# Projecting the late pairs' keys and queries in float32 from each head's own 64 rows

## The chip, the cores and the metric

The kernel runs on one core of a Trainium2 chip. The metric is the time of one execution on the device, in microseconds (us); a smaller one is better. The engines are PE (matrix multiplications, with PEld for its weight loads), DVE, ACT and POOL (arithmetic on vectors) and SP (which issues most of the transfers).

## The reference

Linear attention with a feature map, followed by a gated feed-forward network (FFN) over the heads put side by side. There are 8 batches, 8 heads, 576 tokens, 64 numbers a head; 128 features before the map's two signs; 4608 tokens of 512 go through an FFN of 1536.

```python
def phi(x):
    proj = np.einsum('bhsd,df->bhsf', x, w_phi)
    proj = proj - np.max(np.abs(proj), axis=-1, keepdims=True)
    return np.concatenate([np.exp(proj), np.exp(-proj)], axis=-1)
q_p, k_p = (phi(q), phi(k))
kv = np.einsum('bhsf,bhsd->bhfd', k_p, v)
z = np.sum(k_p, axis=2)
num = np.einsum('bhsf,bhfd->bhsd', q_p, kv)
den = np.einsum('bhsf,bhf->bhs', q_p, z)[..., None] + 1e-06
...
g = x @ w_gate
silu = g * (1.0 / (1.0 + np.exp(-g)))
val = x @ w_val
return (silu * val @ w_out).astype(np.float32)
```

The change concerns `proj`, the product of q and of k with `w_phi`, whose contraction is 64 long.

## The kernel before, in words

**Pairs.** Attention works on pairs of heads, 32 of them, numbered batch by batch. A pair's two heads lie one above the other: head 0 in rows (partitions) 0 to 63, head 1 in rows 64 to 127 of `kin` (keys) and `qin` (queries), tokens along the columns. The first 8 pairs are early, the other 24 late.

**Keys.** Tokens are cut into five blocks; four have 128 tokens of each head, and the fifth holds the last 64 tokens of both heads, each in its own rows with zeros beside them. Blocks 0 and 1, blocks 2 and 3, and block 4 are the three entries of `GROUPS`. An early pair multiplies a block of `kin` (the stationary operand) with `wbd`, 256 columns wide: `w_phi` twice on the diagonal, zeros elsewhere, so that one matmul over all 128 rows gives both heads' features. Block 4 goes with `wst`, `w_phi` twice one above the other. These operands are float32. Late pairs from pair 9 on split the keys: ACT copies them to a narrower format, float32r (`k_hi`, line 417), DVE takes the rest (`k_lo`, line 419), and three matmuls (high by high, high by low, low by high; lines 434 to 444) replace the float32 one. After the projection DVE takes the largest magnitude (`kmax`) and subtracts it (`ksub`), ACT takes two exponentials, and PE adds the values up in the bank `kv` (`values`, lines 463 to 474).

**Queries.** For late pairs the features lie in the rows and tokens in the columns. Each head's 64 rows are split into a high part (ACT, line 553) in its own rows and a low part (DVE, line 555) in the other head's rows, so that one matmul over 128 rows takes both parts; a second one has the weights' low part. Tokens come in two halves of 288 (`SH`), so a head has two steps of two matmuls, and each step's result is copied out by ACT (line 568). DVE then finds the largest magnitude over the features, ACT takes the exponentials, and PE multiplies them with the summed values (`numerators`, lines 612 to 620).

**FFN.** Tokens go in 12 chunks of 384. Chunks 0 to 5 use products of split float32r operands in three terms each (`first` into the banks `gv`, `second` into the banks `o`), chunks 6 to 11 go two at a time by a Strassen scheme (from line 976). In the late pairs' part of the program chunks 1 to 5 stand beside attention.

**Order.** The order is not that of the code. `Plan` (lines 65 to 165) holds steps, each with an engine, a cost in ns, the steps it waits for and a rank, and plays them through: an engine that is free takes the ready step of the lowest rank, and the instructions are written in that order. On PE attention ranks ahead of the FFN, whose steps fill what is left; if nothing is ready, a matmul of zeros (`nil`) is written. A step with `take` needs a bank of PSUM, a step with `give` returns it. There are two work banks, and for early pairs the three `o` banks besides.

Of the kernel before, what the change touches and what calls it, by code (L numbers as in the profile page):

```python
# [10 lines left out]
F32R = mybir.dt.float32r  # L11
# [6 lines left out]
P = 128  # L18
S = 576
# [45 lines left out]
class Plan:  # L65
# [28 lines left out]
    def run(self):  # L94
# [11 lines left out]
        def start(e):  # L106
            nonlocal n, wire
            held = []
            got = None
            while ready[e]:  # L110
                key, s = heapq.heappop(ready[e])
                if s.take is not None and not self.free and not (s.early and self.extra):
                    held.append((key, s))
                    continue
                got = s
                break
# [10 lines left out]
            s = got  # L127
            if s.take is not None:
                self.bank[s.take] = (self.extra if s.early and self.extra else self.free).pop(0)
            s.fn()  # L130
# [41 lines left out]
def dve(n):  # L172
    return 150 + 1.04 * n
# [10 lines left out]
def act(n):  # L184
    return 190 + 0.86 * n
# [11 lines left out]
def favor_attention_moe(ctx: ExitStack, tc: tile.TileContext, qT, kT, v, w_phi, wg, wv, wo, out):  # L197
# [10 lines left out]
    def sb(name, shape, dtype=F32, n=None):  # L208
        if n is None:
            return pool.tile(shape, dtype, name=name, tag=name)  # L210
        return [pool.tile(shape, dtype, name=f"{name}{i}", tag=f"{name}{i}") for i in range(n)]


    wbd_hi, wbd_lo = sb("wbd_hi", [P, 2 * NF], F32R), sb("wbd_lo", [P, 2 * NF], F32R)
    wst_hi, wst_lo = sb("wst_hi", [P, NF], F32R), sb("wst_lo", [P, NF], F32R)
    w1_hi = sb("w1_hi", [P, 2, NK, P], F32R, NFT)
# [26 lines left out]
    def view(tag, shape, dtype=F32, when=0, o=None):  # L243
        n = size(shape)
        if o is None:
            o = filled.get((tag, when), 0)
            filled[tag, when] = o + n
        assert o + n <= ROOM[tag], (tag, when, o + n)
        made = lambda: shaped(space(tag, when, F32 if dtype is U32 else dtype)[:, o:o + n], shape, dtype)
        return made if when else made()  # L250
# [3 lines left out]
    qx, qe = ([view("m1", [2, S]) for _ in range(2)] for _ in range(2))  # L254
    kp = [view("m1", [2, 2, 2, NF]) for _ in range(2)]
    kvs = [view("m2", [4 * P]) for _ in range(2)]
# [14 lines left out]
    we, wa = ([t[:, i * DM:(i + 1) * DM] for i in range(2)] for t in shared[2:])  # L271
    ks, qs = view("a1", [2, SK], F32R, 1), view("a1", [2, S], F32R, 1)
    for t, shape in ((kin, [SK]), (qin, [SK]), (vf, [5, 2, D2])):
# [20 lines left out]
    make_identity(nc, ident)  # L294
    for hi, lo, w in ((wbd_hi, wbd_lo, wbd), (wst_hi, wst_lo, wst)):
        nc.scalar.copy(hi, w)
        nc.vector.tensor_tensor(out=lo, in0=w, in1=hi, op=ALU.subtract)
    nc.gpsimd.memset(vf[0][:, :, :, D:], 1.0)
# [73 lines left out]
    def attention(i, rank):  # L372
        b, pr = divmod(i, NPAIR)
        plan.early = early = i < EARLY_PAIRS
        plain = i <= EARLY_PAIRS
        j = i % 2
# [36 lines left out]

        if plain:
            k_ready = k_in
        else:
            k_hi = add("ACT", act(SK), lambda: nc.scalar.copy(ks()[:, 0], get(kin[one])),
                       [*k_in, last.get(("khi", i - 1)), *weights_done], rk)
            k_lo = add("DVE", dve(SK), lambda: vec.tensor_tensor(
                out=ks()[:, 1], in0=get(kin[one]), in1=ks()[:, 0], op=ALU.subtract), [k_hi], rk)  # L420
            k_ready = [k_hi, k_lo]
            last["kin", i] = k_lo
        kv_steps = []
        for g, (t0, t1) in enumerate(GROUPS):

            tail = t1 == 5
            w = t1 - t0
            n = 1 if tail else 2 * w
            key = ("k", i, g)
            buf = (3 * i + g) % 2  # L430
            view = lambda key=key, n=n: work[plan.bank[key]][:, :n * NF].rearrange("p (n f) -> p n f", f=NF)
            room = kp[buf].rearrange("p t h s f -> p (t h) s f")[:, :n]

            def project(t0=t0, t1=t1, key=key, tail=tail):
                o = work[plan.bank[key]]
                for t in range(t0, t1):
                    c = slice(t * P, (t + 1) * P)
                    acc = o[:, :NF] if tail else o[:, (t - t0) * 256:(t - t0 + 1) * 256]
                    if plain:
                        matmuls([(acc, get(kin[one])[:, c], wst if tail else wbd, True, True)])  # L440
                    else:
                        khi, klo = (ks()[:, n, c] for n in range(2))
                        w_hi, w_lo = (wst_hi, wst_lo) if tail else (wbd_hi, wbd_lo)
                        matmuls([(acc, khi, w_hi, True, False), (acc, khi, w_lo, False, False), (acc, klo, w_hi, False, True)])

            width = NF if tail else 256
            kproj = add("PE", w * (pe32(width) if plain else 3 * pe(width)), project, k_ready, rk, take=key)
            m = km[(3 * i + g) % len(km)][:, :n]
# [13 lines left out]

            def values(t0=t0, t1=t1, room=room, tail=tail):
                kv_open[0] = not tail
                if tail:
                    for k in range(2):
                        nc.tensor.matmul(ps_kv[:, 2 * k * D2:2 * (k + 1) * D2], room[:, 0, k],  # L467
                                         get(vf[one])[:, 4].rearrange("p h d -> p (h d)"), start=False, stop=k == 1)
                    return
                for t in range(t0, t1):  # L470
                    for h in range(2):
                        for k in range(2):
                            o = ps_kv[:, (2 * k + h) * D2:(2 * k + h + 1) * D2]
                            nc.tensor.matmul(o, room[:, 2 * (t - t0) + h, k], get(vf[one])[:, t, h], start=t + h + k == 0, stop=False)  # L474

            kv = add("PE", 2 * n * pe32(D2), values, [e1, *v_in, last.get(("kv", i - 1)), *kv_steps[-1:]], rk)
            last["kp", 3 * i + g] = kv
            kv_steps.append(kv)
        last["khi", i] = kproj
        if plain:  # L480
            last["kin", i] = kproj
        last["vf", i] = kv_steps[-1]
# [18 lines left out]
        if early:  # L501
            for g, (t0, t1) in enumerate(GROUPS):
# [15 lines left out]

                pj = add("PE", pe32(NF) if tail else w * pe32(256), project, q_in, rank, take=key)
                mx = add("DVE", dve(u * NF), lambda u=u, m=m, view=view: vec.tensor_reduce(  # L520
# [16 lines left out]

                tn = add("PE", u * 108, turn, [qc], rank, take=key2)
                last["qy", n] = tn
# [9 lines left out]
        else:  # L549
            copies, q_lo = [], []  # L550
            for h in range(2):
                ra, rb = rows(h)
                hi = add("ACT", act(S), lambda h=h, ra=ra: nc.scalar.copy(qs()[ra, h], get(qin[one])[ra, :S]),
                         [*q_in, last.get(("qs", h, i - 1)), *weights_done], rq)
                lo = add("DVE", dve(S), lambda h=h, ra=ra, rb=rb: vec.tensor_tensor(
                    out=qs()[rb, h], in0=get(qin[one])[ra, :S], in1=qs()[ra, h], op=ALU.subtract), [hi], rq)
                q_lo.append(lo)
                for part in range(2):
                    key = ("q", i, h, part)
                    c = slice(part * SH, (part + 1) * SH)  # L560

                    def project(h=h, c=c, key=key):
                        acc = work[plan.bank[key]][:, :SH]
                        x = qs()[:, h, c]
                        matmuls([(acc, wst_hi, x, True, False), (acc, wst_lo, x, False, True)])

                    pj = add("PE", 2 * pe(SH), project, [lo], rq, take=key)
                    copies.append(add("ACT", act(SH), lambda h=h, c=c, key=key: nc.scalar.copy(
                        qx[j][:, h, c], work[plan.bank[key]][:, :SH]), [pj, *use("qx")], freeing, give=key))
                last["qs", h, i] = pj  # L570
            last["qin", i] = q_lo[-1]
            blocks = lambda t: flat(t).rearrange("p (a j) -> p a j", j=32)
# [10 lines left out]
            def over_groups():  # L583
# [6 lines left out]

            mx = [add("DVE", dve(S), f, [turns[h]], rm) for h, f in enumerate(per_head(largest))]
            mg = add("DVE", 6 * 170, over_groups, [*mx, last.get(("back", i - 1))], rm)
            back = [add("DVE", dve(S), f, [mg], rm) for f in per_head(lambda h: vec.transpose(
                blocks(qe[j], h), qu[:, cols(h)].rearrange("p (a o) -> p a o", o=1).broadcast_to([P, NBL, 32])))]
# [11 lines left out]
        for h in range(2):  # L606
            for part in range(2):
# [11 lines left out]

                nu = add("PE", 2 * pe32(SH), numerators, [*done[h], *kvc, nu], rn, take=key)  # L620
                free = last.get(("num", i - 1), ())
# [526 lines left out]
```

## Time and profile before

| what | value |
|---|---|
| median of 3 runs | 1263.96 us (1260.27 to 1263.97) |
| the profiled execution | 1263.36 us, span 1261.6 us, granted clock 0.997 |
| PE busy | 1240.2 us (98%), 7008 matmul passes |
| DVE busy | 942.8 us (75%) |
| ACT busy | 687.5 us (54%) |
| POOL busy | 241.5 us (19%) |
| the longest sum of PE waits on one line | 4.9 us in 3 waits (line 1008, for the DVE sums of line 1019) |

A row of the trace names the line, the engine, the operation, the tile written and the tiles read, and the shape. Several tiles share a space, so `m` stands for most tiles of attention and `a` for the split operands and the weights on their way. PE's matmuls overlap at their ends: an instruction's own length is longer than the distance to the next one's start, and that distance is what it costs while PE is busy. The page counts a float32 matmul as two passes and one of float32r as one.

### The profile page before, as it was taken

Reading aid. Unit: us, or ns where it says so; the run is one execution under the profiler, and the core shown is the slowest. Engines: PE = TensorE matmul, PEld = TensorE weight load, DVE = VectorE, ACT = ScalarE, POOL = GpSimd, SP = SyncE. Lnnn points to the kernel's source line nnn. Section 1 sums busy time; section 2 is a strip of 40 time slices with the busy share of each in tenths; the row PEclk is TensorE's granted clock in tenths of the full one; section 3 lists DMA queues with packets and bytes.
Section 4 is the critical chain, followed back from the end, with each engine's and each line's share of the span. In section 5 each row is a group of like instructions: output and inputs, shape, how many; then the busy total and the mean of one; then the engine's idle time right before and its main releaser. Section 6 shows DMA issues by size and latency. Waiting matters only on the chain.

```text
span 1261.6 us, 19300 instructions
## 1 busy us (share of the span) xinstructions
PE 1240.2 (98%) x7008; PEld 1145.5 (91%) x7008; DVE 942.8 (75%) x1674; ACT 687.5 (54%) x1419; POOL 241.5 (19%) x306
## 2 busy tenths in 40 slices
PE   9999999999999999999999999989999999999998
PEld 8887999999888998999999999979998999989997
DVE  7997799998899898999989632476557656575553
ACT  5887333336788787777778522233334433353333
POOL 0000000000000000000000010065565655565550
PEclk9999999999999999999999999999999999999999
DMA  4443355557554433343443244542213322222211
GB/s 137 135 116 99 132 176 173 178 167 211 164 153 123 130 92 114 117 121 114 141 118 97 86 152 151 175 150 76 71 55 111 117 73 76 75 101 75 76 51 51
DMA packets 107312, 149.26 MB, mean 118 GB/s; under 512 B 52048, under 2 KB 61776, under 8 KB 107216
## 3 DMA queue, kind: packets, MB, share of 16 engines
q1 hardware_dynamic: 106752, 147.76, 37.7%
q8 instruction: 55, 0.90, 0.3%
q14 instruction: 41, 0.34, 0.1%
q10 hardware_dynamic: 464, 0.26, 0.1%
HBM read 119.67 MB, written 28.31 MB: 117 GB/s over the span
## 4 chain that ended last, share of the span: by engine, by line
PE 89%; DVE 5%; DMA 2%; ACT 1%; POOL 1%; issue 1%; SPq 0%; DVEq 0%; ACTq 0%; POOLq 0%
PE gv L313 23%; PE gv L1008 19%; PE o L313 19%; PE work L313 17%; PE kv L474 8%; PE kv L313 2%; PE kv L467 1%; POOL a L915 1%; POOL a L920 1%; DVE m L953 0%; DVE xl L957 0%; PE o L536 0%; DMA x_dram<-m 0%; DVE m L525 0%; DMA out_dram<-osb 0%
## 5 line engine op out<-in xcount | busy, mean ns | idle before, releaser
L313 PE MATMUL gv<-xh,w_hi 128*128 128x384 f32 x576 | 200.6, 348 | 1.4 <-DVE th L744 1.4
L313 PE MATMUL gv<-xh,w_lo 128*128 128x384 f32 x576 | 193.3, 336 | 0.0
L313 PE MATMUL gv<-xl,w_hi 128*128 128x384 f32 x576 | 193.3, 336 | 0.0
L1008 PE MATMUL gv<-xh,m 128*128 128x384 f32 x504 | 150.6, 337 | 3.1 <-ACT m L1016 2.5
L915 POOL TENSOR_TENSOR a<-w_hi,m 128x256 f32<-128x256 f32 x48 | 40.3, 869 | 500.5 <-DMA m<-wlo_dram 492.7
L915 POOL TENSOR_TENSOR a<-w_hi,w_lo 128x256 f32<-128x256 f32 x96 | 85.7, 922 | 193.6 <-DMA w_lo<-wlo_dram 169.9
L920 POOL TENSOR_TENSOR a<-a 128x256 f32<-128x256 f32 x144 | 114.9, 798 | 8.5
L313 PEld LDWEIGHTS gv<-xh,w_hi 128*128 128x128 f32 x576 | 108.3, 188 | 5.1 <-DVE th L744 2.0
L313 PE MATMUL work<-m,m 128*128 128x288 f32 x408 | 110.2, 408 | 1.7 <-ACT m L624 1.7
L313 PE MATMUL o<-w_hi,hh 128*128 128x512 f32 x270 | 111.3, 412 | 0.0
L313 PEld LDWEIGHTS gv<-xl,w_hi 128*128 128x128 f32 x576 | 108.3, 188 | 3.1 <-DVE xl L659 0.2
L1019 DVE TENSOR_TENSOR a<-gv,a 128x384 f32<-128x384 f32 x72 | 39.9, 554 | 93.9 <-PE gv L1008 93.6
L313 PEld LDWEIGHTS gv<-xh,w_lo 128*128 128x128 f32 x576 | 108.1, 188 | 0.0
L313 PE MATMUL o<-w_hi,hl 128*128 128x512 f32 x270 | 107.2, 397 | 0.0
L1008 PEld LDWEIGHTS gv<-xh,m 128*128 128x128 f32 x504 | 93.2, 188 | 6.0 <-ACT m L1016 3.1
L313 PE MATMUL o<-w_lo,hh 128*128 128x512 f32 x243 | 95.7, 394 | 0.0
L313 PEld LDWEIGHTS work<-m,m 128*128 128x128 f32 x408 | 75.6, 190 | 19.2 <-ACT m L624 2.0
L742 ACT ACTIVATE th<-gv 128x384 f32<-128x384 f32 x72 | 35.3, 490 | 96.5 <-PE gv L313 93.4
L767 ACT CAST hh<-th 128x384 fp32r<-128x384 f32 x108 | 55.2, 511 | 52.5 <-DVE th L747 39.1
L474 PEld LDWEIGHTS kv<-m,m 128*128 128x128 f32 x640 | 75.9, 192 | 3.6 <-ACT m L458 1.2
L1008 PE MATMUL gv<-xh,w_hi 128*128 128x384 f32 x216 | 73.0, 338 | 4.9 <-DVE a L1019 4.9
L474 PE MATMUL kv<-m,m 128*128 128x66 f32 x640 | 75.5, 273 | 1.3 <-ACT m L458 1.0
(183 smaller groups left out, 2993.9 us busy)
## 6 DMA issues: line engine op xcount, KB each, us to landing
w_lo<-wlo_dram SPq DMA_DIRECT2D x60, 512.0 KB, 3.6
w_lo<-wlo_dram SPq DMA_DIRECT2D x78, 256.0 KB, 3.1
wlo_dram<-w_lo SPq DMA_DIRECT2D x36, 256.0 KB, 2.1
out_dram<-osb SPq DMA_DIRECT2D x30, 256.0 KB, 2.9
a<-in_wg_dram SPq DMA_DIRECT2D x12, 512.0 KB, 3.6
a<-in_wv_dram SPq DMA_DIRECT2D x12, 512.0 KB, 3.6
a<-in_wo_dram SPq DMA_DIRECT2D x12, 512.0 KB, 3.7
m<-wlo_dram SPq DMA_DIRECT2D x12, 512.0 KB, 3.5
```

Source lines behind the costliest of these rows:

```text
L313: nc.tensor.matmul(o, l, r, start=a, stop=z)
L467: nc.tensor.matmul(ps_kv[:, 2 * k * D2:2 * (k + 1) * D2], room[:, 0, k], get(vf[one])[:, 4].rearrange("p h d -> p (h d)"), start=False, st ...
L474: nc.tensor.matmul(o, room[:, 2 * (t - t0) + h, k], get(vf[one])[:, t, h], start=t + h + k == 0, stop=False)
L742: s1 = add("ACT", act(CH), lambda: nc.scalar.activation(t_, ps_gv[0][:, :CH], AF.Tanh, scale=0.5), [ends[0], th_free[j]], FIRST)
L767: s4 = add("ACT", act(CH), lambda: nc.scalar.copy(get(hh[b]), th[j]), [made, hid_free[b]], FIRST)
L915: gp.tensor_tensor(out=full()[:, block(n)], in0=hi[:, block(n)], in1=get(low)[:, block(n)], op=ALU.add)
L920: gp.tensor_tensor(out=x[:, block(o)], in0=x[:, block(l)], in1=x[:, block(r)], op=ALU.subtract)
L1008: nc.tensor.matmul(o[:, :CH], l, r, start=begin and i == 0, stop=i == len(terms) - 1, skip_group_check=True)
L1019: return add("DVE", dve(CH), lambda: vec.tensor_tensor(out=snap[n](), in0=bank_c[:, :CH], in1=snap[n](), op=ALU.add), after, FIRST)
```

## The change

Late pairs are no longer split. Keys of the four full blocks are projected by eight float32 matmuls, each over one head's 64 rows, against the 64 rows of `wst` that hold `w_phi` for that head; head 0's results go to one work bank, head 1's to the other, and heads alternate. Block 4 stays a matmul over 128 rows, now in float32. Queries are projected by float32 matmuls of 288 columns over one head's 64 rows, the two heads of a half in one step, again into two banks. The steps' list of banks (`take`) can now hold two, and a step whose banks are not free holds back all later ones that need banks. The four split copies of `w_phi`, the splits of keys and queries and their space go away. Pair 8 takes part too. The build gives a matmul over 64 rows its own strip of PE's array: size 64 by 128, at row 0 or row 64.

```diff
-                if s.take is not None and not self.free and not (s.early and self.extra):
+                if s.take is not None and (saved or len(s.take) > len(self.free) + (len(self.extra) if s.early else 0)):
                     held.append((key, s))
+                    saved = True
                     continue
...
-        if plain:
-            k_ready = k_in
-        else:
-            k_hi = add("ACT", act(SK), lambda: nc.scalar.copy(ks()[:, 0], get(kin[one])),
-                       [*k_in, last.get(("khi", i - 1)), *weights_done], rk)
-            k_lo = add("DVE", dve(SK), lambda: vec.tensor_tensor(
-                out=ks()[:, 1], in0=get(kin[one]), in1=ks()[:, 0], op=ALU.subtract), [k_hi], rk)
...
+                for t in range(4):
+                    for h in range(2):
+                        r = rows(h)[0]
+                        matmuls([(work[plan.bank["k", i, h]][:, t * NF:(t + 1) * NF], x[r, t * P:(t + 1) * P],
+                                  wst[r], True, True)])
+
+            if early:
+                kproj = add("PE", pe32(NF) if tail else 2 * pe32(256), project, k_in, rk, take=[key])
+            elif g != 1:
+                kproj = add("PE", n * pe32(NF), project,
+                            [*k_in, *(last.get(("kp", 3 * i + u - 2)) for u in ((2,) if tail else (0, 1)))], rk,
+                            take=[key] if tail else [key, ("k", i, 1)])
...
-            copies, q_lo = [], []
-            for h in range(2):
-                ra, rb = rows(h)
-                hi = add("ACT", act(S), lambda h=h, ra=ra: nc.scalar.copy(qs()[ra, h], get(qin[one])[ra, :S]),
-                         [*q_in, last.get(("qs", h, i - 1)), *weights_done], rq)
-                lo = add("DVE", dve(S), lambda h=h, ra=ra, rb=rb: vec.tensor_tensor(
-                    out=qs()[rb, h], in0=get(qin[one])[ra, :S], in1=qs()[ra, h], op=ALU.subtract), [hi], rq)
...
-                        matmuls([(acc, wst_hi, x, True, False), (acc, wst_lo, x, False, True)])
...
+            copies = [None] * 4
+            for part in range(2):
+                c = slice(part * SH, (part + 1) * SH)
+                keys = [("q", i, h, part) for h in range(2)]
+
+                def project(c=c, keys=keys):
+                    for h in range(2):
+                        r = rows(h)[0]
+                        matmuls([(work[plan.bank[keys[h]]][:, :SH], wst[r], get(qin[one])[r, c], True, True)])
+
+                pj = add("PE", pe32(SH), project, [*q_in, *use("qx")], rq, take=keys)
```

On PE, a query step of a late pair between the values' last matmuls and the FFN (`gv`) reads so before; `work` with a number is a work bank, `a` the split queries:

```order
L467 MATMUL kv<-m_0_105,m_0_104 128x132 x2
L313 MATMUL work_132<-a_1_2452,wst_hi 128x288
L313 MATMUL work_132<-a_1_2452,wst_lo 128x288
L313 MATMUL work_133<-a_1_2452,wst_hi 128x288
L313 MATMUL work_133<-a_1_2452,wst_lo 128x288
L313 MATMUL gv_129<-xh_98,w_hi_75 128x384
```

After the change the same place on PE has one matmul a head, and the values' matmuls between the two query steps; `m` is now `qin` itself:

```order
L308 MATMUL work_129<-m_0_101,wst 128x288
L308 MATMUL work_128<-m_0_101,wst 128x288
L460 MATMUL kv<-a_1_2516,m_0_100 128x132 x2
L308 MATMUL gv_125<-xh_94,w_hi_69 128x384
L308 MATMUL gv_125<-xl_97,w_hi_69 128x384
L308 MATMUL gv_125<-xh_94,w_lo_91 128x384
```

Four matmuls of two steps have become two of one step, and in a strip of 64 rows each.

On PE, the keys of a late pair before: the first of two such groups, six matmuls into one bank, and the start of the second:

```order
L313 MATMUL work_132<-wbd_hi,a_1_2452 128x256
L313 MATMUL work_132<-wbd_lo,a_1_2452 128x256
L313 MATMUL work_132<-wbd_hi,a_1_2452 128x256 x2
L313 MATMUL work_132<-wbd_lo,a_1_2452 128x256
L313 MATMUL work_132<-wbd_hi,a_1_2452 128x256
L313 MATMUL work_133<-wbd_hi,a_1_2452 128x256
```

And the keys of a late pair on PE after, from the FFN step ahead of them:

```order
L308 MATMUL gv_126<-xh_94,w_hi_69 128x384
L308 MATMUL gv_126<-xl_97,w_hi_69 128x384
L308 MATMUL gv_126<-xh_94,w_lo_91 128x384
L308 MATMUL work_129<-wst,m_0_101 128x128
L308 MATMUL work_128<-wst,m_0_101 128x128
```

The last two rows stand there four times in turn, once a block; all eight matmuls are one step that holds both banks, and FFN matmuls over all rows stand on both sides of it.

More of the change, by code (lines that the diff above doesn't have):

```diff
@@ L108, in start @@
             held = []
-            got = None
+            got, saved = None, False
             while ready[e]:
                 key, s = heapq.heappop(ready[e])
-                if s.take is not None and not self.free and not (s.early and self.extra):
+                if s.take is not None and (saved or len(s.take) > len(self.free) + (len(self.extra) if s.early else 0)):
                     held.append((key, s))
+                    saved = True
                     continue
@@ L127, in start @@
             s = got
-            if s.take is not None:
-                self.bank[s.take] = (self.extra if s.early and self.extra else self.free).pop(0)
+            for t in s.take or ():
+                self.bank[t] = (self.extra if s.early and self.extra else self.free).pop(0)
             s.fn()
@@ L211, in sb @@
         return [pool.tile(shape, dtype, name=f"{name}{i}", tag=f"{name}{i}") for i in range(n)]
-    wbd_hi, wbd_lo = sb("wbd_hi", [P, 2 * NF], F32R), sb("wbd_lo", [P, 2 * NF], F32R)
-    wst_hi, wst_lo = sb("wst_hi", [P, NF], F32R), sb("wst_lo", [P, NF], F32R)
     w1_hi = sb("w1_hi", [P, 2, NK, P], F32R, NFT)
@@ L254, in favor_attention_moe @@
     qx, qe = ([view("m1", [2, S]) for _ in range(2)] for _ in range(2))
-    kp = [view("m1", [2, 2, 2, NF]) for _ in range(2)]
+    kp = [view("m1", [4, 2, NF]) for _ in range(2)]
     kvs = [view("m2", [4 * P]) for _ in range(2)]
@@ L271, in favor_attention_moe @@
     we, wa = ([t[:, i * DM:(i + 1) * DM] for i in range(2)] for t in shared[2:])
-    ks, qs = view("a1", [2, SK], F32R, 1), view("a1", [2, S], F32R, 1)
     for t, shape in ((kin, [SK]), (qin, [SK]), (vf, [5, 2, D2])):
@@ L294, in favor_attention_moe @@
     make_identity(nc, ident)
-    for hi, lo, w in ((wbd_hi, wbd_lo, wbd), (wst_hi, wst_lo, wst)):
-        nc.scalar.copy(hi, w)
-        nc.vector.tensor_tensor(out=lo, in0=w, in1=hi, op=ALU.subtract)
     nc.gpsimd.memset(vf[0][:, :, :, D:], 1.0)
@@ L374, in attention @@
         plan.early = early = i < EARLY_PAIRS
-        plain = i <= EARLY_PAIRS
         j = i % 2
@@ L411, in attention @@
                      before("vf"), rank) for h in range(2)]
-        if plain:
-            k_ready = k_in
-        else:
-            k_hi = add("ACT", act(SK), lambda: nc.scalar.copy(ks()[:, 0], get(kin[one])),
-                       [*k_in, last.get(("khi", i - 1)), *weights_done], rk)
-            k_lo = add("DVE", dve(SK), lambda: vec.tensor_tensor(
-                out=ks()[:, 1], in0=get(kin[one]), in1=ks()[:, 0], op=ALU.subtract), [k_hi], rk)
-            k_ready = [k_hi, k_lo]
-            last["kin", i] = k_lo
-        kv_steps = []
+        kv_steps, kproj = [], None
         for g, (t0, t1) in enumerate(GROUPS):
             tail = t1 == 5
-            w = t1 - t0
-            n = 1 if tail else 2 * w
+            slots = [(4, 0)] if tail else [(t, h) for t in range(t0, t1) for h in range(2)] if early else \
+                [(t, g) for t in range(4)]
+            n = len(slots)
             key = ("k", i, g)
@@ L431, in attention @@
             view = lambda key=key, n=n: work[plan.bank[key]][:, :n * NF].rearrange("p (n f) -> p n f", f=NF)
-            room = kp[buf].rearrange("p t h s f -> p (t h) s f")[:, :n]
+            room = kp[buf][:, :n]
             def project(t0=t0, t1=t1, key=key, tail=tail):
[L435 to L447, printed above, removed]
+                x = get(kin[one])
+                if early or tail:
+                    o = work[plan.bank[key]]
+                    for t in range(t0, t1):
+                        c = slice(t * P, (t + 1) * P)
+                        matmuls([(o[:, :NF] if tail else o[:, (t - t0) * 256:(t - t0 + 1) * 256], x[:, c],
+                                  wst if tail else wbd, True, True)])
+                    return
+                for t in range(4):
[9 more added lines that the diff above has]
+                            take=[key] if tail else [key, ("k", i, 1)])
             m = km[(3 * i + g) % len(km)][:, :n]
@@ L461, in attention, with values @@
             last["km", 3 * i + g] = ksub
-            def values(t0=t0, t1=t1, room=room, tail=tail):
+            def values(g=g, slots=slots, room=room, tail=tail):
                 kv_open[0] = not tail
@@ L469, in values @@
                     return
-                for t in range(t0, t1):
-                    for h in range(2):
-                        for k in range(2):
-                            o = ps_kv[:, (2 * k + h) * D2:(2 * k + h + 1) * D2]
-                            nc.tensor.matmul(o, room[:, 2 * (t - t0) + h, k], get(vf[one])[:, t, h], start=t + h + k == 0, stop=False)
+                for m, (t, h) in enumerate(slots):
+                    for k in range(2):
+                        o = ps_kv[:, (2 * k + h) * D2:(2 * k + h + 1) * D2]
+                        nc.tensor.matmul(o, room[:, m, k], get(vf[one])[:, t, h], start=g + m + k == 0, stop=False)
             kv = add("PE", 2 * n * pe32(D2), values, [e1, *v_in, last.get(("kv", i - 1)), *kv_steps[-1:]], rk)
@@ L478, in attention @@
             kv_steps.append(kv)
-        last["khi", i] = kproj
-        if plain:
-            last["kin", i] = kproj
+        last["kin", i] = kproj
         last["vf", i] = kv_steps[-1]
@@ L517, in project @@
                                  (o[:, (t - t0) * 256:(t - t0 + 1) * 256], x, wbd, True, True)])
-                pj = add("PE", pe32(NF) if tail else w * pe32(256), project, q_in, rank, take=key)
+                pj = add("PE", pe32(NF) if tail else w * pe32(256), project, q_in, rank, take=[key])
                 mx = add("DVE", dve(u * NF), lambda u=u, m=m, view=view: vec.tensor_reduce(
@@ L536, in turn @@
                             nc.tensor.transpose(o[:, (h * w + t) * P:(h * w + t + 1) * P], y[:, 2 * t + h], ident)
-                tn = add("PE", u * 108, turn, [qc], rank, take=key2)
+                tn = add("PE", u * 108, turn, [qc], rank, take=[key2])
                 last["qy", n] = tn
@@ L549, in attention @@
         else:
-            copies, q_lo = [], []
-            for h in range(2):
-                ra, rb = rows(h)
-                hi = add("ACT", act(S), lambda h=h, ra=ra: nc.scalar.copy(qs()[ra, h], get(qin[one])[ra, :S]),
-                         [*q_in, last.get(("qs", h, i - 1)), *weights_done], rq)
-                lo = add("DVE", dve(S), lambda h=h, ra=ra, rb=rb: vec.tensor_tensor(
-                    out=qs()[rb, h], in0=get(qin[one])[ra, :S], in1=qs()[ra, h], op=ALU.subtract), [hi], rq)
[L557 to L564, printed above, removed]
-                        matmuls([(acc, wst_hi, x, True, False), (acc, wst_lo, x, False, True)])
[L567 to L571, printed above, removed]
+            copies = [None] * 4
[7 more added lines that the diff above has]
+                pj = add("PE", pe32(SH), project, [*q_in, *use("qx")], rq, take=keys)
+                for h in range(2):
+                    copies[2 * h + part] = add("ACT", act(SH), lambda h=h, c=c, key=keys[h]: nc.scalar.copy(
+                        qx[j][:, h, c], work[plan.bank[key]][:, :SH]), [pj, *use("qx")], freeing, give=keys[h])
+            last["qin", i] = pj
             blocks = lambda t: flat(t).rearrange("p (a j) -> p a j", j=32)
@@ L589, in over_groups @@
                 vec.tensor_copy(qu[64:128], qu[0:64])
-            mx = [add("DVE", dve(S), f, [turns[h]], rm) for h, f in enumerate(per_head(largest))]
+            mx = [add("DVE", dve(S), f, [turns[h], last.get(("mg", i - 1))], rm) for h, f in enumerate(per_head(largest))]
             mg = add("DVE", 6 * 170, over_groups, [*mx, last.get(("back", i - 1))], rm)
+            last["mg", i] = mg
             back = [add("DVE", dve(S), f, [mg], rm) for f in per_head(lambda h: vec.transpose(
@@ L618, in numerators @@
                     matmuls([(o, l, r, m == 0, m == len(terms) - 1) for m, (l, r) in enumerate(terms)])
-                nu = add("PE", 2 * pe32(SH), numerators, [*done[h], *kvc, nu], rn, take=key)
+                nu = add("PE", 2 * pe32(SH), numerators, [*done[h], *kvc, nu], rn, take=[key])
                 free = last.get(("num", i - 1), ())
```

## The prediction

> **What bounds the kernel now.** I read the page's busy times and chain first, then busy time by stage, then the waits of PE, and last PE's timeline, since durations of pipelined matmuls overlap and only the distance from start to start is a price.
>
> ```profile
> PE 1240.2 (98%) x7008; PEld 1145.5 (91%) x7008; DVE 942.8 (75%) x1674; ACT 687.5 (54%) x1419; POOL 241.5 (19%) x306
> PE 89%; DVE 5%; DMA 2%; ACT 1%; POOL 1%; issue 1%; SPq 0%; DVEq 0%; ACTq 0%; POOLq 0%
> ```
>
> PE carries the span and 89% of the chain that ended last. The next rows are busy times by stage: 0 to 150 holds the early pairs, 150 to 410 the weights' decoding and the first late pairs, 410 to 720 the other late pairs beside chunks 2 to 5, 720 to 820 chunk 5 alone.
>
> ```profile
> 0.00:150.00 150.00, 142.99 (x863) 128.51 (x864) 125.00 (x243) 101.38 (x233) 1.34 (x13) 0.99 0.42 121
> 150.00:410.00 260.00, 260.00 (x1464) 241.51 (x1463) 235.76 (x455) 146.24 (x298) 0.59 (x5) 1.00 0.53 169
> 410.00:720.00 310.00, 308.02 (x1949) 285.38 (x1948) 278.95 (x529) 234.70 (x513) 0.00 (x0) 1.00 0.38 113
> 720.00:820.00 100.00, 100.00 (x524) 93.24 (x524) 35.56 (x59) 27.55 (x52) 6.05 (x8) 1.00 0.49 157
> ```
>
> PE (first pair of columns after the length) is busy throughout where the late pairs run, at the full clock (1.00). All that PE waits for between 150 and 820 us is one row:
>
> ```profile
> PE work L313 <- ACT m L624: 2.0, 2, 1.7
> ```
>
> Attention is ready about 100 us before the last chunk that PE fills the time with (720 against 820), so its own latency is covered. What counts is how long PE is occupied by the projections, before and after; every microsecond there moves the end by as much. The sum stands against the profiled execution, 1263.36 us (span 1261.6), 0.05% under the median of 1263.96.
>
> **What is removed on PE.** PE's timeline around one late pair, columns start, length, instruction; key blocks, the last key block, queries:
>
> ```profile
> 534.03 0.28 PE L313 MATMUL work<-wbd_hi,a 128*128 128x256 f32 x1
> ...
> 535.46 0.39 PE L313 MATMUL o<-w_hi,hh 128*128 128x512 f32 x1
> ...
> 538.07 0.22 PE L313 MATMUL work<-wst_hi,a 128*128 128x128 f32 x1
> ...
> 538.76 0.34 PE L313 MATMUL gv<-xh,w_lo 128*128 128x384 f32 x1
> ```
>
> ```profile
> 527.53 0.29 PE L313 MATMUL work<-a,wst_hi 128*128 128x288 f32 x1
> ...
> 528.06 0.34 PE L313 MATMUL gv<-xh,w_hi 128*128 128x384 f32 x1
> ```
>
> The 12 split key matmuls take 535.46 - 534.03 = 1.43 us. The last block's 3 end two gv slots of 0.17 before 538.76, so 0.35 us. Four query matmuls take 0.53, eight 1.06. A pair costs 2.84 us, the 23 pairs from pair 9 on 65.3. Pair 8 has unsplit keys already, of the early pairs' kind:
>
> ```profile
> 119.44 1.02 PE L313 MATMUL work<-wbd,m 128*128 128x256 f32 x4
> 120.30 0.27 PE L536 MATMUL o<-ident,m 128*128 128x128 f32 x1
> ```
>
> Float32 makes two passes of each matmul (x4 are two blocks): 0.86 us for two blocks, 1.72 for four, 0.22 for the last block (below) and 1.06 for its queries: 3.0 us. Removed in all: 68.3 us.
>
> **What is added on PE.** Float32 passes have prices in the numerators (288 columns) and in the values (66):
>
> ```profile
> 529.11 2.10 PE L313 MATMUL work<-m,m 128*128 128x288 f32 x8
> 530.83 0.55 PE L313 MATMUL gv<-xh,w_hi 128*128 128x384 f32 x1
> 531.22 0.34 PE L313 MATMUL gv<-xl,w_hi 128*128 128x384 f32 x1
> 531.39 0.34 PE L313 MATMUL gv<-xh,w_lo 128*128 128x384 f32 x1
> ...
> 539.45 3.68 PE L474 MATMUL kv<-a,m 128*128 128x66 f32 x32
> ...
> 542.94 0.38 PE L313 MATMUL work<-a,wst_hi 128*128 128x288 f32 x1
> ```
>
> The gv matmul after the eight passes holds one 0.17 slot before 531.22, so eight passes are 531.22 - 0.17 - 529.11 = 1.94 us, 0.24 each, twice the 0.13 of a split matmul of that width. A pass of 66 columns takes 3.49 / 32 = 0.11, which its columns alone (0.24 x 66 / 288 = 0.055) don't explain: the weight load sets it. For 128 columns both give 0.11. A late pair now has 16 key passes of 128 columns, 2 for the last block (0.22 us, whole rows), and 8 query passes of 288.
>
> No row shows two strips at work. The bounds: strips one after the other cost 16 x 0.11 + 8 x 0.24 + 0.22 = 3.90 us a pair, 93.6 for 24 pairs, 25.3 more than is removed. Strips fully side by side cost half of the 24 strip passes, 2.06 a pair, 49.4 in all, 18.9 less. I take the middle form. Starts in the timeline keep the program's order, and a head's second pass uses the same strip as its first; so head 1 begins when head 0's second pass does. A query step is then three slots (0.72), a pair 1.44; the eight key matmuls nine slots of 0.11 (0.99). With 0.22 that is 2.65 a pair, 63.6 in all: 4.7 us gained.
>
> **The change of strips.** Each of the 3 strip steps of a pair lies between matmuls over all 128 rows, so 24 x 3 x 2 = 144 times PE goes from one form to the other. No row of before has such a change. If it is free it costs 0. If PE must empty and refill, the nearest row is a stall:
>
> ```profile
> 476.30 0.34 PE L313 MATMUL gv<-xh,w_lo 128*128 128x384 f32 x1
> 478.37 2.21 PE L313 MATMUL work<-m,m 128*128 128x288 f32 x8 [1.73 <-ACT m L624]
> 480.20 0.55 PE L313 MATMUL gv<-xh,w_hi 128*128 128x384 f32 x1
> 480.59 0.33 PE L313 MATMUL gv<-xl,w_hi 128*128 128x384 f32 x1
> ```
>
> After a standstill the same eight passes and the gv slot take 2.22 us instead of 2.11: 0.11 us for a weight load that nothing hides. Emptying adds what a gv matmul lasts beyond its slot, 0.34 - 0.17 = 0.17. So a change costs 0 to 0.28 us, 0 to 40.3 in all. I take 0.11 (15.8 us): the refill is a row of this trace, while the emptying may lie under the next load. The Trainium skill, "TensorEngine Tiling (Array Packing)", section "Key Properties", says that going over to another tiling mode, not merely another tile, drains TensorE. It speaks against the change and gives no time; no run shown so far has a second mode to agree or differ. By it the sum would be +11 to +36, without it -5.
>
> **What is off the path.** The splits leave ACT and DVE:
>
> ```profile
> L553 ACT CAST a<-m 64x576 fp32r<-64x576 f32 x24 | 16.1, 672 | 0.3
> L553 ACT CAST a<-a 64x576 fp32r<-64x576 f32 x24 | 16.1, 670 | 0.2
> L417 ACT CAST a<-a 128x640 fp32r<-128x640 f32 x12 | 8.6, 714 | 0.0
> L417 ACT CAST a<-m 128x640 fp32r<-128x640 f32 x11 | 7.9, 718 | 0.2 <-PE work L313 0.2
> ...
> L555 DVE TENSOR_TENSOR a<-a,a 64x576 fp32r<-64x576 f32 x24 | 18.1, 753 | 0.7
> L555 DVE TENSOR_TENSOR a<-m,a 64x576 fp32r<-64x576 f32 x24 | 18.1, 753 | 0.9
> L419 DVE TENSOR_TENSOR a<-a,a 128x640 fp32r<-128x640 f32 x12 | 9.8, 817 | 0.5 <-ACT a L417 0.3
> L419 DVE TENSOR_TENSOR a<-m,a 128x640 fp32r<-128x640 f32 x11 | 8.9, 811 | 0.1
> ...
> L568 ACT COPY m<-work 128x288 f32<-128x288 f32 x96 | 35.2, 403 | 9.1 <-PE work L313 8.1
> ```
>
> That is 48.7 us of ACT and 54.9 of DVE, worth at most the 2.0 us that PE waits there; taken as 0, because PE's own work covers them. The DMAs and POOL keep their number.
>
> Each strip step now takes both work banks and the second query step needs both back. Two copies at 0.40, after the 0.17 that the last matmul lasts on, make 0.98 us; the shortest filling between the two in the new order is six gv matmuls and four value passes, 6 x 0.17 + 4 x 0.11 = 1.46. Taken as 0; if ACT came as much as 0.3 late every time, 24 x 0.3 = 7 us.
>
> The order of the first 150 us moves too, since pair 8 no longer waits for the weights and a step that finds too few banks holds back those behind it. PE has 7 us idle there; three either way, taken as 0.
>
> Sum: -68.3 + 63.6 + 15.8 = +11.1 us, 1263.4 + 11.1 = 1274.5 us.
>
> **Rivals.**
> Full overlap, change of strips nearly free: faster. All 24 strip passes run in pairs, 18.9 us saved, 1244.5 us. It decides as long as a change costs under 18.9 / 144 = 0.13 us. For it: the two heads use separate rows and separate banks, and nothing in the code makes one wait for the other. Against it: each head has two passes one behind the other in its own strip, and a query step has only two matmuls to interleave. The rule in the Trainium skill, "TensorE: Matmul & The Clock Gate", section "Part 3: Packing small matmuls — row/col tiling", has strips start some 4 ns apart; by it this is the case.
>
> Three slots, change free: -4.7 us, 1258.7 us, at the edge of what can be told from no change (0.3%, 3.8 us). For it: the trace has no stop between float32 and split matmuls. Against it: those are the same rows.
>
> Full emptying at each change: -4.7 + 40.3 = +35.6, 1299 us. For it: the stall above shows what a fresh start costs. Against it: it assumes that even the weight load waits.
>
> The strips don't overlap at all (the change doesn't do what it says): +25.3 us, 1288.7 with free changes, 1304.5 with 0.11 each. For it: the weight loads of the values, 0.11 apart on one engine, show no two loads at once. Against it: those loads use the same rows, so they had to follow each other.
>
> **How the numbers follow.** The forecast (three slots, 0.03 to 0.2 a change: 1263 to 1287) has 0.40, full emptying 0.13, no overlap 0.17, full overlap 0.18, three slots and free 0.12. Faster by over 0.3% takes full overlap and two thirds of the last: 0.26. Within 0.3%: the rest of that and the low end of the forecast, 0.12. Slower: 0.62. The range runs from 1247, which leaves out full overlap with changes under 0.02 us, to 1300, which leaves out no overlap with paid changes; the forecast's own range is 1263 to 1287.
>
> **What would show it.** In the timeline of the new kernel: the start of head 1's first pass against head 0's second (together, or 0.24 later); a query step from its first start to the next gv slot at 0.72 (three slots), 0.48 or 0.96, each plus two changes; the eight key matmuls at 0.99 or 1.76; a gap before and after each strip step. PE should still be busy in 150 to 820, and ACT and DVE some 49 and 55 us lighter. I am wrong if PE waits for the query copies, if the first 150 us move by more than three, or if a strip pass costs another time than a pass over all rows.

## The result and the profile after

The changed kernel takes 1275.01 us (median of 4 runs, 1273.58 to 1279.43) against 1262.9 for the kernel before (median of 4 runs): ratio 1.0107, 95% interval 1.0088 to 1.0125. Forecast were 1274.5 us, slower. The number is right; the rows show that two of its terms were not, and that they made up for each other by luck.

The profiled execution has a span of 1274.6 us, 13.0 more than before. Busy times from its page, busy time by stage (the late pairs now end near 735 us), then all that PE waits for between 150 and 840 us:

```profile
PE 1254.2 (98%) x7092; PEld 1121.4 (88%) x7092; DVE 890.3 (70%) x1601; ACT 644.8 (51%) x1346; POOL 241.8 (19%) x306
```

```profile
150.00:410.00 260.00, 260.00 (x1495) 235.26 (x1494) 226.02 (x442) 129.21 (x265) 0.59 (x5) 1.00 0.54 170
410.00:735.00 325.00, 324.41 (x2004) 273.32 (x2003) 231.20 (x456) 198.00 (x443) 0.00 (x0) 1.00 0.38 115
```

```profile
PE work L308 <- ACT m L608: 0.6, 2, 0.4
PE o L308 <- ACT osb L798: 0.4, 1, 0.4
```

PE is still the bound, and the copies of the queries (line 552) keep nobody waiting there. DVE is 52.5 us lighter and ACT 42.7, and PE, busy throughout, gains nothing by it. In PE's timeline a key step (16 passes in strips) and a query step (4 passes) stand so:

```profile
526.12 0.39 PE L308 MATMUL o<-w_hi,hl 128*128 128x512 f32 x1
526.44 1.16 PE L308 MATMUL work<-wst,m 64*128 64x128 f32 x16
527.53 0.44 PE L308 MATMUL gv<-xh,w_hi 128*128 128x384 f32 x1
527.81 0.34 PE L308 MATMUL gv<-xl,w_hi 128*128 128x384 f32 x1
...
552.91 0.34 PE L308 MATMUL gv<-xh,w_lo 128*128 128x384 f32 x1
553.18 0.76 PE L308 MATMUL work<-m,wst 64*128 64x288 f32 x4
553.86 0.50 PE L308 MATMUL o<-w_hi,hh 128*128 128x512 f32 x1
554.20 0.39 PE L308 MATMUL o<-w_lo,hh 128*128 128x512 f32 x1
```

Take the query step. The gv matmul's slot of 0.17 ends at 553.08, yet the strips start at 553.18: 0.10 us of nothing. On the way out the first o matmul starts at 553.86 and the next 0.34 later, where o matmuls follow each other at 0.23: 0.11 us for a weight load that nothing hides. The step in all is 554.20 - 0.23 - 553.08 = 0.89 us. Two slots of 0.24 are 0.48, so each of the two changes of form costs 0.20. Four passes therefore take two slots: the two heads run fully side by side. The key step is 527.81 - 0.17 - 526.35 = 1.29 us, eight slots of 0.112 and again two changes of 0.20.

A narrow cut of the same timeline shows the side by side directly: only what starts by 553.19 is listed, and two passes of the four have.

```profile
553.18 0.51 PE L308 MATMUL work<-m,wst 64*128 64x288 f32 x2
```

A late pair is 1.29 + 0.22 + 2 x 0.89 = 3.29 us, 24 pairs 79.0 us, against 68.3 removed: +10.7. The forecast had 63.6 + 15.8 = 79.4.

The other place that moved is the early part. Busy time by stage for 100 to 150 us, of the changed kernel and of the one before, and two waits of PE, longer after (first two rows) than before (last two):

```profile
100.00:150.00 50.00, 45.33 (x254) 38.26 (x253) 34.58 (x70) 31.33 (x74) 0.00 (x0) 0.93 0.27 78
```

```profile
100.00:150.00 50.00, 45.72 (x266) 40.65 (x266) 37.35 (x73) 27.06 (x62) 0.00 (x0) 1.00 0.35 107
```

```profile
PE kv L466 <- ACT m L451: 1.9, 1, 1.9
PE kv L466 <- ACT m L452: 1.8, 2, 1.6
```

```profile
PE kv L474 <- ACT m L458: 1.0, 1, 1.0
PE kv L474 <- ACT m L459: 0.2, 1, 0.2
```

PE waits 3.7 us for the exponentials of keys where it waited 1.2, and its granted clock (the column after POOL, a share of the full clock) falls from 1.00 to 0.93 in this stretch. Pair 8 now stands here, since its queries need no split and so no longer wait for the weights.

### The profile page after: what moved, and what is told of

The parts are those of the page before. It is cut to its first block, busy times and chain, and to the rows that moved or that the text cites. A ratio compares the mean times of both kernels' runs of the same rounds, so it can differ in the third digit from the quotient of the medians.

```text
span 1274.6 us, 19263 instructions
## 1 busy us (share of the span) xinstructions
PE 1254.2 (98%) x7092; PEld 1121.4 (88%) x7092; DVE 890.3 (70%) x1601; ACT 644.8 (51%) x1346; POOL 241.8 (19%) x306
## 4 chain that ended last, share of the span: by engine, by line
PE 90%; DVE 4%; ACT 2%; DMA 1%; POOL 1%; issue 1%; SPq 0%; DVEq 0%; ACTq 0%; POOLq 0%
PE gv L308 23%; PE o L308 19%; PE gv L992 19%; PE work L308 17%; PE kv L466 8%; PE kv L308 2%; PE kv L460 1%; POOL a L899 1%; POOL a L904 1%; PE o L526 0%; DVE m L937 0%; DVE xl L941 0%; DMA a<-in_wo_dram 0%; DMA a<-in_wg_dram 0%; DMA w_lo<-wlo_dram 0%
## 5 line engine op out<-in xcount | busy, mean ns | idle before, releaser
L308 PE MATMUL gv<-xh,w_hi 128*128 128x384 f32 x576 | 203.9, 354 | 0.4 <-DVE th L728 0.4
L308 PE MATMUL o<-w_hi,hh 128*128 128x512 f32 x270 | 115.2, 427 | 0.4 <-ACT osb L798 0.4
L466 PE MATMUL kv<-m,m 128*128 128x66 f32 x640 | 78.1, 278 | 3.8 <-ACT m L451 1.9
L451 ACT ACTIVATE m<-m 128x512 f32<-128x512 f32 (+1 forms) x96 | 50.0, 521 | 62.7 <-DVE m L447 62.4
```

The lines of the kernel that those rows point to most:

```text
L308: nc.tensor.matmul(o, l, r, start=a, stop=z)
L451: e0 = add("ACT", act(n * NF), lambda x=room: nc.scalar.activation(x[:, :, 0], x[:, :, 1], AF.Exp), [ksub], rk)
L466: nc.tensor.matmul(o, room[:, m, k], get(vf[one])[:, t, h], start=g + m + k == 0, stop=False)
```

## The experiments

Each time stands against the kernel before on the same chip. First, each half alone.

**Keys alone.** The queries' branch is that of before (with its split `wst` and `qs`), and the plan writes no matmul of zeros into the bank `kv`.

```diff
...
-                        matmuls([(work[plan.bank[keys[h]]][:, :SH], wst[r], get(qin[one])[r, c], True, True)])
...
+                        matmuls([(acc, wst_hi, x, True, False), (acc, wst_lo, x, False, True)])
...
```

> Keys in strips as in the changed kernel, queries split as before. Theory (strips overlap fully, each change of form costs 0.20 us): the key step measures 1.29 us with its two changes (526.35 to 527.64) and the last block 0.22, against 1.78 before; 23 pairs save 0.27 each and pair 8 0.43, so 6.6 us faster than before, about 1256 us. Rival (the loss comes from steps that hold both banks and from the new order of the early part, not from the query strips): still 2 to 6 us slower than before, 1265 to 1269 us.

Measured: 1260.2 us against 1263.98, ratio 0.9967, interval 0.9956 to 0.9979. Faster, as the theory had it, by 3.8 us instead of 6.6. In the profile, part of the gain is given back at the start of the Strassen stage. Its busy time by stage, that of the kernel before at the same place, and a wait there that before doesn't have:

```profile
815.00:850.00 35.00, 28.92 (x135) 26.39 (x135) 28.23 (x32) 14.74 (x25) 25.14 (x24) 0.90 0.39 130
```

```profile
820.00:850.00 30.00, 25.72 (x132) 23.15 (x131) 21.64 (x26) 11.71 (x21) 19.84 (x21) 1.00 0.50 158
```

```profile
PE gv L1003 <- DVE th L739: 3.1, 1, 3.1
```

PE is idle for 6.1 us of these 35 and at a clock of 0.90; before, it is idle for 4.3 of 30 at the full clock.

**Queries alone.** The keys' branch is that of before.

```diff
...
-                        matmuls([(work[plan.bank["k", i, h]][:, t * NF:(t + 1) * NF], x[r, t * P:(t + 1) * P],
-                                  wst[r], True, True)])
...
+                        matmuls([(acc, khi, w_hi, True, False), (acc, khi, w_lo, False, False), (acc, klo, w_hi, False, True)])
...
```

> Queries in strips as in the changed kernel, keys split as before. Theory: a query step measures 0.89 us with its two changes, a pair 1.78 against 1.06 before; 24 pairs lose 0.72 each, 17.3 us slower than before, about 1280 us. Rival (banks and early order are to blame): under 8 us slower, since one strip step in three is gone and pair 8's keys are as before.

Measured: 1281.44 against 1263.98, ratio 1.0138, interval 1.012 to 1.0157, so 17.5 us slower. The loss is in the queries, more than the whole change loses, and the keys give some back. (The early stretch is disturbed here as well, its clock over the first 150 us 0.97 against 0.99 before, so not all of the 17.5 are strips.)

**How far PE looks ahead.** All key blocks of head 0 first:

```diff
-                for t in range(4):
-                    for h in range(2):
+                for h in range(2):
+                    for t in range(4):
```

> The changed kernel with the eight key matmuls in another order: all four blocks of head 0, then all four of head 1. If PE starts passes strictly in the program's order, the strips overlap only where the heads meet, the step takes 16 slots of 0.11 instead of 8, 24 x 0.9 = 21 us slower than the changed kernel, about 1296 us. If PE starts a pass of the free strip ahead of waiting ones, the step stays near 1.29 us and the time near 1275 us. The pairs of starts 7 ns apart in the changed kernel fit both.

Measured: 1291.29 against 1263.98, ratio 1.022, interval 1.02 to 1.0241; 27.3 us over before, some 15 over the changed kernel. Neither expectation: the step in the timeline is

```profile
547.53 0.40 PE L308 MATMUL o<-w_hi,hl 128*128 128x512 f32 x1
547.86 1.71 PE L308 MATMUL work<-wst,a 64*128 64x128 f32 x16
549.49 0.44 PE L308 MATMUL gv<-xh,w_hi 128*128 128x384 f32 x1
549.77 0.34 PE L308 MATMUL gv<-xl,w_hi 128*128 128x384 f32 x1
```

so 549.77 - 0.17 - 547.76 = 1.84 us, less two changes 1.43: 13 slots of 0.11. Three passes of head 0 found a partner among the eight of head 1. PE does start passes of the free strip ahead of waiting ones, but here only about three places ahead; alternating heads is what gives the full overlap. 24 x (1.84 - 1.29) = 13.2 us of the 15.

**No strips.** The same steps, banks and order over all 128 rows:

```diff
-                        matmuls([(work[plan.bank["k", i, h]][:, t * NF:(t + 1) * NF], x[r, t * P:(t + 1) * P],
-                                  wst[r], True, True)])
+                        matmuls([(work[plan.bank["k", i, h]][:, t * NF:(t + 1) * NF], x[:, t * P:(t + 1) * P],
+                                  wbd[:, h * NF:(h + 1) * NF], True, True)])
...
-                        matmuls([(work[plan.bank[keys[h]]][:, :SH], wst[r], get(qin[one])[r, c], True, True)])
+                        matmuls([(work[plan.bank[keys[h]]][:, :SH], wbd[:, h * NF:(h + 1) * NF], get(qin[one])[:, c], True, True)])
```

> The changed kernel with the same steps, banks, order and number of passes, but every key and query matmul over all 128 rows, with the block-diagonal weights (zeros for the other head): no strips, so no change of form and no overlap. Theory: no gaps; keys 16 x 0.112 = 1.79 us against 1.29, queries 8 x 0.242 = 1.94 against 1.78; 24 x 0.66 = 15.8 us slower than the changed kernel, about 1291 us. Rival (the gaps of 0.10 us around the steps are waits for banks or copies): they stay, and with them 144 x 0.20 = 29 us more, about 1320 us.

Measured: 1294.15 against 1263.98, ratio 1.0239, interval 1.0219 to 1.0259, some 18 us over the changed kernel. A query step in its timeline:

```profile
540.04 0.34 PE L308 MATMUL gv<-xh,w_lo 128*128 128x384 f32 x1
540.22 1.13 PE L308 MATMUL work<-a,wbd 128*128 128x288 f32 x4
541.19 0.56 PE L465 MATMUL kv<-m,m 128*128 128x66 f32 x4
```

The step starts 0.18 after the gv matmul, its plain slot, with the same wait for two banks ahead of it; its four passes take 0.97. The gap goes with the strips, so it is no wait for a bank.

**The price of a change, in time.** One of the four key blocks goes over all rows, the third (two changes more a pair) or the fourth (as many as the changed kernel):

```diff
-                        r = rows(h)[0]
+                        r = slice(0, P) if t == 2 else rows(h)[0]
+                        w = wbd[:, h * NF:(h + 1) * NF] if t == 2 else wst[r]
...
-                                  wst[r], True, True)])
+                                  w, True, True)])
```

> The changed kernel, but the third of the four key blocks of a late pair goes over all 128 rows (block-diagonal weights) between blocks in strips. Two more changes of form a pair, and four passes of 0.112 where two slots were. Theory (0.20 us a change): 24 x (0.41 + 0.22) = 15 us slower than the changed kernel. Rival (the 0.20 us belongs to the start and end of a step, to its semaphores, not to the form): 24 x 0.22 = 5.4 us slower, the same as the kernel with the fourth block.

> The same with the fourth block over all 128 rows: as many changes of form as the changed kernel has, and the same passes as with the third block. Both theories: 24 x 0.22 = 5.4 us slower than the changed kernel; by the theory some 9.7 us faster than with the third block (48 changes of 0.20), by the rival the same.

Measured beside the changed kernel itself, run again:

> The changed kernel as it is, for comparison on the same chip: 1273 to 1277 us, 10 to 13 us over the kernel before.

| kernel | median us | before | ratio, interval |
|---|---|---|---|
| changed, again | 1275.97 | 1263.12 | 1.01 (1.0078 to 1.0122) |
| fourth block over all rows | 1280.63 | 1263.12 | 1.0134 (1.0113 to 1.0156) |
| third block over all rows | 1289.12 | 1263.12 | 1.0206 (1.0182 to 1.0229) |

The fourth block costs 4.7 us, the third 13.2, and the 48 changes between them 8.5, 0.18 each. The third block's step in the timeline, then the fourth's:

```profile
543.49 0.40 PE L308 MATMUL o<-w_hi,hl 128*128 128x512 f32 x1
543.82 0.72 PE L308 MATMUL work<-wst,a 64*128 64x128 f32 x8
544.46 0.71 PE L308 MATMUL work<-wbd,a 128*128 128x128 f32 x4
545.10 0.49 PE L308 MATMUL work<-wst,a 64*128 64x128 f32 x4
545.52 0.44 PE L308 MATMUL gv<-xh,w_hi 128*128 128x384 f32 x1
545.80 0.33 PE L308 MATMUL gv<-xl,w_hi 128*128 128x384 f32 x1
```

```profile
542.89 0.40 PE L308 MATMUL o<-w_hi,hl 128*128 128x512 f32 x1
543.22 0.94 PE L308 MATMUL work<-wst,a 64*128 64x128 f32 x12
544.09 0.71 PE L308 MATMUL work<-wbd,a 128*128 128x128 f32 x4
544.55 0.42 PE L308 MATMUL gv<-xh,w_hi 128*128 128x384 f32 x1
544.81 0.33 PE L308 MATMUL gv<-xl,w_hi 128*128 128x384 f32 x1
```

545.80 - 0.17 - 543.72 = 1.91 us against 544.81 - 0.17 - 543.12 = 1.52: the same passes, 0.39 more for two changes that stand inside one step, with no wait shown at any of its rows.

**Pair 8.** Its queries wait for the weights again (and no zeros go into `kv`):

```diff
-                pj = add("PE", pe32(SH), project, [*q_in, *use("qx")], rq, take=keys)
+                pj = add("PE", pe32(SH), project, [*q_in, *use("qx"), *(weights_done if i == EARLY_PAIRS else ())], rq, take=keys)
```

> The changed kernel with the queries of pair 8 held back until the weights are decoded, as before (and without the zero matmuls into the bank kv). Theory: of the 13.0 us between the two profiled spans the strips explain 10.3; the rest is in the first 150 us, where PE waits 3.5 us for the exponentials of pair 8's keys' and runs at half clock for 6.8 us, since pair 8 now stands there. Then this kernel is 2 to 4 us faster than the changed one. Rival (the rest lies in the strips' surroundings later on): no difference.

Measured: 1269.37 against 1263.12, ratio 1.0054, interval 1.0035 to 1.0073: 6.6 us faster than the changed kernel. The stretch from 100 to 150 us, and what is left of the two waits:

```profile
100.00:150.00 50.00, 46.24 (x279) 41.19 (x277) 37.28 (x72) 27.36 (x61) 0.00 (x0) 1.00 0.38 116
```

```profile
PE kv L466 <- ACT m L451: 1.1, 1, 1.1
PE kv L466 <- ACT m L452: 0.2, 1, 0.2
```

The clock is whole again and 2.4 us of waiting are gone. So half of the time that the change loses comes with the place that pair 8 got and not with the strips. The direction is the theory's, the size twice what it expected. The six zero matmuls into `kv` (1.6 us busy in the changed kernel, where nothing else was ready) went at the same time and were not tried apart.

**Keeping the gain of the keys.** On top of the keys alone, and for comparison on the kernel before, the loads of the Strassen stage's first operands start three FFN steps earlier:

```diff
-                 [*(x_stored[x] for x in need), *temp_free[n], *(spread[n - 7:][:1] if c == PAIRS else ())], NEXT))
+                 [*(x_stored[x] for x in need), *temp_free[n], *(spread[n - 10:][:1] if c == PAIRS else ())], NEXT))
```

> Keys in strips and queries split, as in the kernel with keys only, but the loads of the Strassen stage's first operands three FFN steps earlier (n - 10 for n - 7). In the keys-only profile PE reaches the end of chunk 5 7.7 us ahead of before and the end of the program only 0.8 ahead: DVE's operand sums run beside POOL's weight sums at 815 to 829 us, chunk 5's last gate waits 3.1 us for DVE, and PE runs at half clock for two stretches of 3.4 us. Theory: with the sums out of the way the gain is kept, 1255 to 1258 us. Rival (the stage's start is bound by POOL in any case): as the keys-only kernel, 1260 us.

> The kernel before with the same earlier loads and nothing else: whether the shift by itself gains. In the profile before, PE waits 4.3 us in 820 to 850 us for POOL's weight sums and DVE's. Theory: these waits belong to POOL, so no difference from before within 0.2%. Rival: 2 to 4 us faster, and then the shift, not the keys, would be what the kernel above gains.

Measured: 1259.61 against 1263.41 (0.9967, interval 0.9952 to 0.9982) and 1263.03 against 1263.41 (0.9995, interval 0.9977 to 1.0012). The shift does nothing for either, and the wait for `th` is still there with it, 3.4 us. So the rival's time came out, but that POOL binds the stage is not shown. Keys alone, with or without the shift, is the fastest version here, faster than both kernels.

**The granted clock.** Each run lists the clock that PE was granted, as a mean over its span. Span times this clock is an estimate of the time at full clock, since PE is busy for 98% of the span. Medians over all runs of a kernel, against before on the same chip:

| kernel | time, us | at full clock, us |
|---|---|---|
| keys alone | -3.8 | -7.0 |
| keys alone, loads earlier | -3.8 | -7.2 |
| queries alone | +17.5 | +15.4 |
| changed, again | +12.9 | +10.5 |
| fourth block over all rows | +17.5 | +15.8 |
| third block over all rows | +26.0 | +25.3 |
| pair 8 late | +6.3 | +7.9 |

At full clock the keys alone gain 7.0 us where the theory had 6.6: what their time lacks is clock (0.995 in the mean of the twelve runs, 0.997 before). Why the clock is lower there is open. Pair 8's place costs 2.5 us at full clock, about the 2.4 us of waits, and the rest of its 6.6 is clock. The third and the fourth block lie 9.5 us apart, 0.20 for each of the 48 changes.

## Why the prediction was right, and where it was not

- **Bound.** Right: PE stays busy from 150 to 735 us, and what was taken off ACT and DVE (42.7 and 52.5 us, forecast some 49 and 55) brought nothing there.
- **What is removed, 68.3 us.** No run measures it by itself, but nothing speaks against it: with the key step as measured it gives 6.6 us for the keys alone, and 7.0 came out at full clock. The price of a pass stands: with strips' changes taken off, 0.112 us for 128 columns and 0.24 for 288.
- **Three slots, 63.6 us.** Too high. The step that failed was "starts in the timeline keep the program's order": a pass of the free strip starts ahead of a waiting one, so the strips overlap fully, 49.4 us, the rival's figure. The rule of the Trainium skill that gave it ("TensorE: Matmul & The Clock Gate", "Part 3: Packing small matmuls — row/col tiling", starts some 4 ns apart) agrees with the two slots measured for four passes.
- **The change of strips, 15.8 us.** Too low. The refill of 0.11 us is there as taken, and the emptying, which I let lie under the next load, costs 0.10 of its own (forecast 0 to 0.17): 0.20 a change, 144 x 0.20 = 29 us. The drain that the Trainium skill states ("TensorEngine Tiling (Array Packing)", "Key Properties") is in the trace: 0.10 us of nothing ahead of a strip step, which the kernel without strips does not have.
- The two misses are 14 us down and 13 up, so 79.0 us came out for 79.4. That the forecast met the time is luck: neither term was right. The rival "full overlap" put its turning point at 0.13 us a change; at 0.20 it loses, as it said.
- **The first 150 us, taken as 0, three either way.** Too small: with pair 8's queries held back the kernel is 6.6 us faster. That is more than three, one of the prediction's own signs of being wrong; the other two, a wait of PE for the query copies between 150 and 820 us and another price of a strip pass, did not come. The prediction saw that pair 8 moves and did not follow what its keys' exponentials would do to PE and its clock.
- These two together, 10.7 and 6.6, are more than the 12.9 us measured beside them. The clock tells part of it: at full clock the change without pair 8's move loses 7.9 us, not 6.3. PE's idle time in the late pairs' part (2.0 before, 0.6 after) covers 1.4 of the 2.8 us that 10.7 is still too many; the rest is of the size of the intervals and stays open.

## What to carry to other kernels

Small contractions in row strips give their factor of two, for weight loads and passes, if matmuls alternate between strips; but each turn from whole rows to strips or back cost about 0.20 us here, in key and query steps alike. Divide that by the length of the run of strip work: sixteen short passes (0.90 us saved of 1.79, 0.41 paid) earn it, four long ones (0.48 saved of 0.97, 0.41 paid) hardly do, and against split operands at twice the speed they lose. And when a step loses a dependency, look where the planner puts it next: moving one pair forward cost 6.6 us here, beside the strips' 10.7. Some 4 of the 6.6 were granted clock, so compare span times clock before looking for a limit in a time that came out too long.

## What was not expected of the hardware

A float32 matmul's two passes on one strip don't hold up the other strip: two passes have started within 0.01 us of the step's begin, though the program has head 0's matmul first. The look-ahead is short, 13 slots instead of 8 when four matmuls of one head come first.

A wait of under two microseconds can be followed by half the clock. Busy times of three stretches of the changed kernel, columns as for the stages:

```profile
126.00:129.00 3.00, 1.38 (x10) 1.08 (x8) 2.76 (x9) 2.92 (x7) 0.00 (x0) 1.00 0.00 0
129.00:134.00 5.00, 5.00 (x32) 5.00 (x30) 4.23 (x8) 1.44 (x4) 0.00 (x0) 0.62 0.00 0
134.00:137.00 3.00, 3.00 (x13) 3.00 (x12) 1.68 (x5) 1.69 (x5) 0.00 (x0) 0.50 0.05 11
```

PE idles for 1.6 us of the first three, and its clock is at half by 134 us, where it is busy throughout. The length of the wait alone doesn't decide it. The stall at 478 us in the kernel before, 1.73 us long, had no such consequence: its stage is at 1.00. The kernel with the third block over all rows has the same wait of 1.62 us in the same place, before 127.87 us (the changed kernel before 128.58), and its clock over 100 to 150 us is 1.00. What decides it is open.
